# A spatial gate by one Strassen level, logits summed on TensorE, and engine orders written out as lists

## The chip, the core and the metric

The kernel runs on one core of one Trainium2 chip. The time is the device time of one execution in microseconds (us): the median of three runs was 236.79 us (236.54 to 237.99). The engines named below are PE (TensorE, matrix products), DVE (VectorE, elementwise), ACT (ScalarE, activations and PSUM evictions), POOL (GpSimd) and SP (SyncE, here an issuer of DMA transfers). Each engine works through its own list of instructions in order and meets the others through semaphores.

## The reference

One token sequence x of 2048 x 512 (bf16) is normalised, and two branches are added to it.

```python
xn = layernorm(x)                                   # 2048 x 512
# A: 32 heads of 16, each token looks at 8 tokens: itself, 2, 4, ... 14 back
q, k, v = split(xn @ wqkv)
logits  = sum_d q[s] * k[s - 2w] / 4                # w = 0..7, masked below token 0
A = (softmax_w(logits) @ v[s - 2w]) @ wo
# B: gated MLP with a spatial matrix w_sp (2048 x 2048)
z  = gelu(xn @ w_in)                                # 2048 x 1792
z1, z2 = z[:, :896], layernorm(z[:, 896:])
g  = w_sp @ z2 + b_sp[:, None]                      # 2048 x 896
B  = (z1 * g) @ w_out
out = x + A + B
```

The largest product is w_sp @ z2: 2048 x 2048 x 896.

## The kernel before, in words

Python code builds a list of tasks (`T(engine, function, reads, writes, est, name)`), finds their dependences from the tiles they read and write, and a planner (`schedule`) sets the order on each engine from estimated durations, priorities and four short prefixes. `emit` then writes each engine's instructions in that order with semaphore waits. All large tiles lie in one SBUF tensor, `arena`; the eight PSUM banks are the tensor `ps`.

The work in stages, with the lines that the profile names:

- **Start.** Nine dummy matmuls (L570) while x arrives. Each of 16 token blocks of 128 goes through DVE statistics (L598, L601), a power on POOL for 1/sqrt (L603) and the DVE normalisation (L605). Blocks 0 to 3 are transposed on PE (L620), the others by a DMA transpose (L609), into xnT.
- **Projections.** For each of four column blocks j of 512 tokens: Q and K with features on partitions (L665, evicted two banks at once by ACT at L673), V with tokens on partitions (L647, L651, stored to a DRAM scratch at L654), and z2 (L785, gelu with accumulated sums at L790, squares at L812, statistics at L818 to L828, power on POOL L831, normalisation on DVE L834). The last 16 columns of K are copied by POOL (L679) as a halo for the next block. z1 is computed with features on partitions (L802, L807).
- **Logits.** For each j DVE multiplies Q with eight shifted K views, one chunk of four feature groups at a time (L689, 128 x 4096), adds the four products in three adds (L694), a DMA transpose of 1 MB (L706) turns features to the free axis, and two more DVE adds finish the sum over features (L714, L717). The softmax follows (L727 to L766, the exponential on ACT at L746). The attention weights go to DRAM and back (L768, L772 on POOL's queue) to change their token order.
- **Gate.** Four transposing loads of w_sp, 512 output tokens each, 2 MB (L841), two buffers. For each of 7 feature groups and 4 token groups: ACT writes the bias to a PSUM bank (L902), 16 matmuls of 128 x 512 add the product (L908), and DVE multiplies the bank into z1 (L915).
- **Attention output.** For each j and parity, ACT's queue loads nine shifted views of V from DRAM, DVE multiplies them by the weights (L933), adds them (L937 twice, L941), and SP issues a DMA transpose (L946).
- **Output.** For each token block ACT writes x into a PSUM bank (L969), 4 + 7 matmuls add A and B (L974, L978), ACT evicts (L987), and ACT's queue stores.

The names in the new lists follow the tasks: `P1_3` is product 1 of token-block pair 3, `lg2_1` the second logits sum of block j = 2.

Of the kernel before, what the change touches and what calls it, by code (L numbers as in the profile page):

```python
# [14 lines left out]
class Plan:  # L15
# [79 lines left out]
    def schedule(self, lookahead=64, slack=120.0, dma_bw=300.0, xbar_bw=190.0,  # L95
                 dma_lat=1700.0, issue_ns=None, inv_tol=None, sw_bias=1300.0, verbose=False):
        inv_tol = inv_tol or {"dve": 2400.0}
        issue_ns = issue_ns or {"sp": 650.0, "act": 650.0, "pool": 660.0}
        pending = {e: {} for e in ENGS}
        for t in self.tasks:  # L100
            pending[t.eng].setdefault(t.prio[0], []).append(t)
        for e in ENGS:
            for c in pending[e]:
                pending[e][c].sort(key=lambda t: t.prio)
        byname = {t.name: t for t in self.tasks}
        before = {}
        for names in self.orders:
            for a, b in zip(names, names[1:]):
                assert byname[a].eng == byname[b].eng
                before.setdefault(byname[b], []).append(byname[a])  # L110
        eng_free = {e: 0.0 for e in ENGS}
        dma_free = {e: 0.0 for e in ENGS}
        dma_glob = [0.0]
        order = {e: [] for e in ENGS}
        remaining = len(self.tasks)

        def lat(d, t):
            if d.dma is not None:
                return 150.0
            if d.eng == t.eng:  # L120
                return 35.0
            return 210.0 if d.eng == "pe" else 80.0

        cur_tbl = [None]

        def dur(t):
            if t.dma is not None:
                return issue_ns.get(t.eng, 650.0)
            if t.tbl is not None and t.tbl != cur_tbl[0]:
                return t.est + 1300.0  # L130
            return t.est

        while remaining:
            best = None
            for e in ENGS:
                pl = []
                for c in pending[e]:
                    pl.extend(pending[e][c][:lookahead])
                if not pl:
                    continue  # L140
                cands = []
                for t in pl:
                    ok = all(p.start is not None for p in before.get(t, ()))
                    ready = 0.0
                    for d in t.deps:
                        if d.end is None:
                            ok = False
                            break
                        r = d.end + lat(d, t)
                        if r > ready:  # L150
                            ready = r
                    if ok:
                        st_ = max(eng_free[e], ready + t.margin)
                        if t.tbl is not None and t.tbl != cur_tbl[0] and cur_tbl[0] is not None:
                            st_ += sw_bias
                        cands.append((st_, t))
                if not cands:
                    continue
                pick = None
                pool_c = list(cands)  # L160
                while pool_c:
                    mn = min(c[0] for c in pool_c)
                    near = [c for c in pool_c if c[0] <= mn + slack]
                    P = min(near, key=lambda c: (c[1].prio, c[0]))
                    pend = P[0] + dur(P[1])
                    viol = False
                    for c in cands:
                        if c[1].prio[0] < P[1].prio[0] and pend > c[0] + inv_tol.get(e, 300.0):
                            viol = True
                            break  # L170
                    if not viol:
                        pick = P
                        break
                    pool_c.remove(P)
                if pick is None:
                    pick = min(cands, key=lambda c: (c[1].prio[0], c[0], c[1].prio))
                if best is None or (pick[0], pick[1].prio) < (best[0], best[1].prio):
                    best = pick
            if best is None:
                raise RuntimeError("scheduler stuck (dependency cycle?)")  # L180
            st, t = best
            e = t.eng
            if t.tbl is not None and t.tbl != cur_tbl[0] and cur_tbl[0] is not None:
                st -= sw_bias
            t.start = st
            if t.dma is not None:
                iss = issue_ns.get(e, 650.0)
                t.eng_end = st + iss
                bw = xbar_bw if t.dma.get("xbar") else dma_bw
                xs = max(st + 0.5 * iss, dma_glob[0])  # L190
                xe = xs + t.dma["nbytes"] / bw
                dma_glob[0] = xe
                t.end = max(xe, st + iss) + dma_lat
            else:
                t.eng_end = st + dur(t)
                t.end = t.eng_end
                if t.tbl is not None:
                    cur_tbl[0] = t.tbl
            eng_free[e] = t.eng_end
            pending[e][t.prio[0]].remove(t)  # L200
            order[e].append(t)
            remaining -= 1
        self.order = order
        self.makespan = max(t.end for t in self.tasks)
        if verbose:
            self.report()
        return order

    def report(self, buckets=10):
        print("makespan(est) = %.1f us" % (self.makespan / 1000.0))  # L210
        for e in ENGS:
            busy = sum((t.eng_end - t.start) for t in self.order[e])
            last = max((t.eng_end for t in self.order[e]), default=0.0)
            print("  %-4s tasks=%5d busy=%7.1f us (%.0f%%) last_end=%7.1f us" % (
                e, len(self.order[e]), busy / 1000.0, 100.0 * busy / max(self.makespan, 1.0), last / 1000.0))
# [90 lines left out]
DEFAULT_CFG = dict(  # L306
    xdma=4,
    fill=1,
    warm=9,
    fill0=2,  # L310
    perm=0,
# [3 lines left out]
def build_kernel(nc, A_x, A_wqkv, A_wo, B_x, B_w_in, B_w_sp, B_b_sp, B_w_out, out, report=False, sched_kw=None,  # L315
# [4 lines left out]
    assert D == 512 and S % 512 == 0  # L320
    NB = S // 128
    NJ = S // 512
    FH = 896
    HF = FH // 2
    FC = FH // 128
    W = 8
    KP = 16
    FILL = cfg["fill"]
    XDMA = cfg["xdma"]
    PERM = cfg["perm"]  # L330
# [4 lines left out]
    ascr = nc.dram_tensor("ascr", (S, 256), BF).ap()  # L335
# [9 lines left out]
    WSL = NB * 512  # L345
    NWS = min(2, NJ)
    NPB = 4
    NQ = 2
    off = {}
    base = 0  # L350
    for k, v in dict(xin=0, xn=2048, wqk=4096, wv_raw=8192, xin2=10240, Vn=12288).items():
        off[k] = base + v
    off["wT"] = base
    base += NWS * WSL
    off["OT"] = base
    off["xnT"] = base
    base += 4 * S
    off["w_in"] = base
    off["w_out"] = base
    off["wo"] = base + FC * 512  # L360
    base += 7168
    off["QT"] = base
    off["KT"] = base + 4 * 512 * NQ
    ksz = 2 * 4 * (512 + KP)
    off["pb"] = off["KT"] + ksz
    off["Vs"] = off["QT"]
    off["On"] = off["pb"]
    off["xres"] = off["On"] + 2048
    off["yout"] = off["xres"] + 2048
    base = off["pb"] + NPB * 4096  # L370
    off["Ve"] = base
    base += 9216
    off["zeros"] = base
    off["Za"] = base
    off["sqj"] = base + 512
    base += 512 + FH
    for name, n in (("z2", NB * FH), ("z1T", FC * S), ("attn", NB * 256), ("R", 128), ("ident", 128),
                    ("maskt", 256), ("mx", 128), ("Zb", 256), ("bbc", S)):
        off[name] = base
        base += n  # L380
        base = (base + 15) & ~15
    ARENA_E = base
# [3 lines left out]
    for name, n in (("prime", 4), ("Z", 128), ("st6", NB * 9),  # L386
                    ("mv", NB * 2), ("vpe", NB), ("rstd", NB), ("s1", 2 * NB), ("s2", NB), ("m2", NB), ("msq", NB),
                    ("vpe2", NB), ("rstd2", NB), ("mhalf", 4)):
        foff[name] = fb
        fb += n  # L390
# [4 lines left out]
    with ExitStack() as es:  # L395
# [13 lines left out]
        def AC(o_, dims):  # L409
            return bass.AP(tensor=ar, offset=o_, ap=[[AR, 128]] + [list(d) for d in dims])  # L410
# [10 lines left out]
        def bank(k):  # L421
            return ps[:, 512 * k: 512 * (k + 1)]
# [17 lines left out]
        for s_ in range(NPB):  # L440
            R1(("pb", s_), "pb", 4096, 4096 * s_)
        for s_ in range(2):
            R1(("On", s_), "On", 1024, 1024 * s_)
# [625 lines left out]
```

## Time and profile before

| | |
|---|---|
| median of three runs | 236.79 us |
| span of the profiled execution, first to last instruction | 236.3 us |
| granted TensorE clock | 1.000 in every window |
| PE busy | 230.9 us, 98% of the span |
| DVE busy | 202.8 us, 86% |
| ACT busy | 117.6 us, 50% |
| POOL busy | 51.8 us, 22% |
| DMA | 41.75 MB in 87,021 packets, mean 177 GB/s |
| first gate matmul | 97.3 us |
| last matmul | about 233.9 us |

The profile gives the span of one execution and no other time for it; the median of the runs is 0.5 us above that span. "Busy" of PE counts modelled ends of pipelined matmuls: one 512-column matmul is listed with 379 ns, but 32 of them in a row take 6.91 us, so one is issued every 216 ns. Where work is summed, the distance from start to start is used, not the listed duration. In a list of groups, the last columns are busy time and mean of one, then the idle time of the engine just ahead of them and who ended it.

### The profile page before, as it was taken

Reading aid. Unit: us, or ns where it says so; the run is one execution under the profiler, and the core shown is the slowest. Engines: PE = TensorE matmul, PEld = TensorE weight load, DVE = VectorE, ACT = ScalarE, POOL = GpSimd, SP = SyncE. Lnnn points to the kernel's source line nnn. Section 1 sums busy time; section 2 is a strip of 40 time slices with the busy share of each in tenths; the row PEclk is TensorE's granted clock in tenths of the full one; section 3 lists DMA queues with packets and bytes.
Section 4 is the critical chain, followed back from the end, with each engine's and each line's share of the span. In section 5 each row is a group of like instructions: output and inputs, shape, how many; then the busy total and the mean of one; then the engine's idle time right before and its main releaser. Section 6 shows DMA issues by size and latency. Waiting matters only on the chain.

```text
span 236.3 us, 2933 instructions
## 1 busy us (share of the span) xinstructions
PE 230.9 (98%) x1094; PEld 109.9 (47%) x1094; DVE 202.8 (86%) x230; ACT 117.6 (50%) x227; POOL 51.8 (22%) x67
## 2 busy tenths in 40 slices
PE   8999999999999999999999999999999799999995
PEld 2454454554554444444444444444444344444553
DVE  4789969998989989997999991799999999999900
ACT  2798488988988978942012132134124134111441
POOL 4447963771690050001301000001000000000000
DMA  6999986290209899696549999999773959912132
GB/s 226 281 356 189 206 223 192 92 178 0 90 3 178 202 249 260 116 247 214 147 96 242 199 215 232 248 182 337 191 206 93 243 147 275 223 23 44 67 89 67
DMA packets 87021, 41.75 MB, mean 177 GB/s; under 512 B 66000, under 2 KB 85856, under 8 KB 87008
## 3 DMA queue, kind: packets, MB, share of 16 engines
q1 hardware_dynamic: 70928, 23.24, 48.4%
q10 hardware_dynamic: 14640, 14.13, 20.4%
q0 software_dynamic: 1440, 4.21, 6.6%
q8 instruction: 8, 0.13, 0.2%
q14 instruction: 5, 0.04, 0.0%
HBM read 20.05 MB, written 5.26 MB: 107 GB/s over the span
## 4 chain that ended last, share of the span: by engine, by line
DVE 50%; PE 31%; DMA 9%; POOL 5%; issue 2%; ACT 2%; DVEq 0%
DVE arena L689 11%; DVE arena L694 9%; DMA arena<-arena 9%; PE ps L908 9%; PE ps L978 6%; DVE arena L933 6%; DVE arena L937 4%; DVE arena L915 4%; POOL fpool L831 4%; PE ps L974 4%; PE ps L665 4%; PE ps L647 3%; PE ps L785 3%; DVE arena L834 2%; DVE arena L717 2%
## 5 line engine op out<-in xcount | busy, mean ns | idle before, releaser
L908 PE MATMUL ps<-arena 128*128 128x512 bf16 x448 | 97.5, 379 | 0.0
L908 PEld LDWEIGHTS ps<-arena 128*128 128x128 bf16 x448 | 43.9, 98 | 52.8 <-ACT ps L902 0.2
L902 ACT ACTIVATE ps<-arena 128x512 f32<-128x512 bf16 x28 | 16.5, 599 | 62.2 <-DVE arena L915 62.1
L933 DVE TENSOR_TENSOR arena<-arena 128x4096 bf16<-128x4096 bf16 x16 | 36.3, 2285 | 0.4
L689 DVE TENSOR_TENSOR arena<-arena 128x4096 bf16<-128x4096 bf16 x16 | 36.1, 2285 | 0.2
L937 DVE TENSOR_TENSOR arena<-arena 128x4096 bf16<-128x4096 bf16 (+1 forms) x16 | 28.1, 1754 | 0.3
L665 PE MATMUL ps<-arena 128*128 128x512 bf16 x128 | 28.3, 379 | 0.0
L694 DVE TENSOR_TENSOR arena<-arena 128x4096 bf16<-128x4096 bf16 x12 | 27.5, 2288 | 0.2
L978 PE MATMUL ps<-arena 128*128 128x512 bf16 (+2 forms) x119 | 27.0, 366 | 0.0
L785 PE MATMUL ps<-arena 128*128 128x448 bf16 x128 | 25.5, 353 | 0.2 <-DVE arena L630 0.2
L802 PE MATMUL ps<-arena 128*128 128x512 bf16 x112 | 24.3, 379 | 0.0
L665 PEld LDWEIGHTS ps<-arena 128*128 128x128 bf16 x128 | 14.5, 113 | 13.1
L915 DVE TENSOR_TENSOR arena<-ps,arena 128x512 bf16<-128x512 f32 x28 | 19.1, 680 | 0.0
L673 ACT ACTIVATE arena<-ps 128x1024 bf16<-128x1024 f32 x16 | 16.3, 1021 | 5.3 <-PE ps L665 4.9
L987 ACT ACTIVATE arena<-ps 128x512 bf16<-128x512 f32 (+1 forms) x16 | 9.4, 585 | 18.4 <-PE ps L978 17.0
L790 ACT ACTIVATE arena<-ps 128x448 bf16<-128x448 f32 x32 | 17.3, 542 | 2.4
L978 PEld LDWEIGHTS ps<-arena 128*128 128x128 bf16 x119 | 13.2, 113 | 11.3
L974 PE MATMUL ps<-arena 128*128 128x512 bf16 (+2 forms) x68 | 16.6, 366 | 1.6 <-DMA arena<-arena 1.6
L785 PEld LDWEIGHTS ps<-arena 128*128 128x128 bf16 x128 | 12.3, 98 | 12.0 <-ACT arena L626 0.7
L807 ACT ACTIVATE arena<-ps 128x512 bf16<-128x512 f32 x28 | 15.9, 595 | 3.2 <-PE ps L802 2.7
L802 PEld LDWEIGHTS ps<-arena 128*128 128x128 bf16 x112 | 10.9, 98 | 13.2
L679 POOL COPY arena<-arena 128x16 bf16<-128x16 bf16 x12 | 14.4, 1207 | 10.9 <-DVE arena L689 9.2
(61 smaller groups left out, 191.2 us busy)
## 6 DMA issues: line engine op xcount, KB each, us to landing
arena<-vscr ACTq DMA_DIRECT2D x8, 1152.0 KB, 7.5
arena<-in_A_x_dram ACTq DMA_DIRECT2D x17, 128.0 KB, 6.0
vscr<-arena POOLq DMA_DIRECT2D x16, 128.0 KB, 2.3
arena<-in_A_x_dram SPq DMA_DIRECT2D x15, 128.0 KB, 4.6
out_dram<-arena ACTq DMA_DIRECT2D x15, 128.0 KB, 1.9
arena<-in_A_wqkv_dram SPq DMA_DIRECT2D x3, 512.0 KB, 5.4
ascr<-arena POOLq DMA_DIRECT2D x4, 256.0 KB, 4.1
arena<-ascr POOLq DMA_DIRECT2D x4, 256.0 KB, 3.5
```

Of the source, the lines that this page charges most:

```text
L665: last = t.matmul(bank(k + which), AC(off["wqk"] + 1024 * dc + col0, [[4, 128]]), AC(off["xnT"] + dc * S + 512 * j, [[1, 512]]), start=(dc ...
L689: T("dve", lambda v: v.tensor_tensor(pbv, qb, kb, ALU.mult), reads=[("QT", c, j), ("KT", c, j), ("KTpad", c, j)], writes=[("pb", s_)], est ...
L694: T("dve", lambda v: v.tensor_tensor(A("pb", 4096, 4096 * a), A("pb", 4096, 4096 * a), A("pb", 4096, 4096 * b), ALU.add), reads=[("pb", b) ...
L785: last = t.matmul(ps[:, 512 * k: 512 * k + HF], AC(off["xnT"] + dc * S + 128 * b, [[1, 128]]), AC(off["w_in"] + 1792 * dc + c0, [[1, HF]]) ...
L790: T("act", (lambda k, hf: lambda a: a.activation(A("z2", HF, FH * b + HF * hf), ps[:, 512 * k: 512 * k + HF], ACTF.Gelu_apprx_tanh, accum_ ...
L802: lastm = t.matmul(bank(k), AC(off["w_in"] + 1792 * dc + 128 * fc, [[1, 128]]), AC(off["xnT"] + dc * S + 512 * j, [[1, 512]]), start=(dc = ...
L908: last = t.matmul(bank(k), AC(off["z2"] + FH * sh + 128 * fc, [[1, 128]]), AC(off["wT"] + WSL * r_ + sh * 512, [[1, 512]]), start=False, s ...
L915: T("dve", lambda v: v.tensor_tensor(uv, bank(k), uv, ALU.mult), reads=[("ps", k)], writes=[("z1T", fc, tc)], est=c_dve(512) + 20, name="u ...
L933: T("dve", (lambda iv, tv, av: lambda v: v.tensor_tensor(tv, iv, av, ALU.mult))(iv, tv, av), reads=[("attn", j), ("Ve", par)], writes=[("V ...
L937: T("dve", (lambda n: lambda v: v.tensor_tensor(AC(off["Vs"], [[4096, 2], [1, n]]), AC(off["Vs"], [[4096, 2], [1, n]]), AC(off["Vs"] + n, ...
L974: t.matmul(po, AC(off["OT"] + 512 * ot_pos(tb) + 128 * cc, [[1, 128]]), AC(off["wo"] + 512 * cc + c0, [[1, n]]), start=False, stop=False, ...
L978: last = t.matmul(po, AC(off["z1T"] + fc * S + t0, [[ts, 128]]), AC(off["w_out"] + 512 * fc + c0, [[1, n]]), start=False, stop=(fc == FC - ...
```

## The change

What it does, part by part:

1. **Order.** The planner is removed. `ORDERS` holds one list of task names for each engine, and `follow` takes them as they stand.
2. **Gate.** The product w_sp @ z2 is done by one level of Strassen's scheme (Winograd's form): the 2 x 2 blocks of w_sp (token halves) and z2 (token halves by feature halves) give 7 products instead of 8. Tokens are on partitions: for each of 8 pairs of token blocks, 7 products `P1` to `P7` of 8 matmuls, 128 x 448 each. DVE forms the sums of w_sp blocks for each pair (`S13`, `S2`, `S4`) and of z2 blocks once (`T1` to `T4`, two groups each), ACT moves partial sums between banks and SBUF (`fk`, `S5`, `S2e`, `Sc`, `S3e`, `g11`, `g21`), DVE adds (`h`), ACT adds the bias (`g12`, `g22`). w_sp comes in 16 transposing loads of 0.5 MB.
3. **z1 and u.** z1 is computed with tokens on partitions too, both halves evicted in one gelu. DVE multiplies in SBUF (`u`, 128 x 896 bf16, 16 times), and SP issues a DMA transpose of each result (`uT`), which the output matmuls read.
4. **Logits.** Two of the three adds for each j stay. The sums over the 128 partitions of a chunk are taken by PE with a 0/1 mask of 32 columns, eight matmuls of 512 columns at four column positions (`lg`), into banks 6 and 7. ACT evicts (`lge`), a DMA transpose of 256 KB (`lgT`) puts tokens on partitions in the order the weights need, so the way through DRAM and L714, L717 go.
5. **Smaller.** z2's gelu takes both halves at once; V tasks are paired; the working PSUM ring has six banks; b_sp is loaded as a 4 KB column tile by POOL (`ldbsp`) and converted by DVE (`bspf`).

```diff
-    def schedule(self, lookahead=64, slack=120.0, ...):
...
+    def follow(self, orders):
+        byname = {t.name: t for t in self.tasks}
+        self.order = {e: [byname[n] for n in orders[e]] for e in ENGS}
...
+ORDERS = dict(
+    pe="""
+warm xTr0 fill0 z2_0_0 xTr1 z2_0_1 z2_1_0 xTr2 z2_1_1 xTr3 z2_2_0 z2_2_1 Q0_0 K0_0 Q0_1 K0_1 z2_3_0 z2_3_1 Q0_3
...
+z2_10_0 z2_8_1 z2_10_1 z2_9_1 z2_9_0 z2_11_1 lg2_0 z2_11_0 V13 V12 Q3_0 V15 K3_0 V14 K3_1 Q3_1 lg2_1 K3_3 Q3_3
+K3_2 z2_12_1 z2_12_0 Q3_2 z2_14_0 z2_14_1 z2_13_1 z2_15_1 z2_13_0 lg3_0 z2_15_0 z1_8_1 z1_8_0 z1_0_1 z1_0_0
+z1_2_0 z1_1_1 z1_10_1 z1_10_0 z1_1_0 z1_2_1 lg3_1 z1_11_0 z1_9_1 z1_9_0 z1_11_1 z1_3_0 z1_3_1 z1_6_0 z1_6_1
+z1_12_1 z1_4_0 z1_4_1 z1_12_0 z1_13_0 z1_14_0 z1_13_1 z1_14_1 z1_5_1 z1_5_0 z1_7_1 z1_7_0 z1_15_0 z1_15_1 P1_0
+P1_1 P5_0 P2_0 P3_0 P5_1 P6_0 P2_1 P7_0 P6_1 P4_0 P7_1 P3_1 P1_2 P1_3 P4_1 P2_2 P6_2 P5_2 P7_2 P3_2 out0_0 P4_2
+P5_3 P2_3 P6_3 P1_4 P3_3 P7_3 out8_0 P6_4 P4_3 P5_4 P2_4 P1_5 out10_0 P7_4 P3_4 P4_4 out2_0 P1_6 P2_5 P6_5 P5_5
...
+    dve="""
+steps0 steps1 zeros bspf bnst0 bnag0 bnst1 norm0 bnag1 xTf0 norm1 bnst2 bnag2 bnst3 norm2 bnag3 bnst5 bnag5
...
+ssub0 zm2 sm3_1 ze2 zv1 ssub1 prod3_1 prod3_0 zq2 zv0 zv2 padd3_1 prod3_2 prod3_3 sz1_0 zn2 sz2_0 zn10 zn6 zn4
+S13_0 zn7 sz3_0 padd3_3 sz1_1 zn3 zn0 srec0 sz2_1 S2_0 zn1 zm3 zn8 zn5 T1_0 sz3_1 T1_1 zn9 zn11 zq3 sattn0 sm1_2
+pv0_0_0 ze3 sm2_2 zv3 sm3_2 S13_1 S4_0 pv0_0_1 zn15 zn14 zn12 zn13 pva2048_0_0 T3_0 T3_1 T2_0 ssub2 T2_1 S2_1
+pva1024_0_0 T4_0 sz1_2 S4_1 srec1 sz2_2 T4_1 h_0 sattn1 sm1_3 sz3_2 srec2 pvc0_0 sattn2 u_0 pv2_0_1 u_8 S13_2
...
+    pool="""
+ldbsp mhalf ident0 ident1 Vzero rstd0 rstd1 rstd2 rstd3 ktpad mlog0 rstd5 rstd4 mlog1 halo0_0 rstd7 rstd6 mask0
...
+            def msum(s_, first, last, n):
+                def mm(t):
+                    for w in range(8):
+                        g, hb = w % 4, w // 4
+                        lm = t.matmul(ps[32 * g: 32 * g + 32, 512 * (6 + hb): 512 * (6 + hb) + 512], mlog,
+                                      A("pb", 512, 4096 * s_ + 512 * w), start=first, stop=last,
+                                      skip_group_check=True, tile_position=(0, 32 * g))
...
+            prod("P1", ba, w0, lambda s: z2m(s, 0), True, [A11] + zr(0, 0))
+            evac("fk", bank(bb, HF), ba, ("ps", bb), scale=-1.0)
+            prod("P5", bc, s0, tm(0), True, [("S1", r_), ("T1", 0), ("T1", 1)])
+            evac("S5", A("Y", HF, HF), bc, ("Y", 1), scale=-1.0)
+            prod("P2", ba, w0 + 1024, lambda s: z2m(8 + s, 0), False, [A12] + zr(8, 0))
+            evac("g11", gz(0), ba, ("G", r_, 0), bias=bt)
+            prod("P6", bb, s0 + 1024, tm(1), False, [("S2", r_), ("T2", 0), ("T2", 1)])
+            evac("S2e", A("X", HF), bb, ("X", 0), scale=-1.0)
+            prod("P3", bc, s0 + 2048, lambda s: z2m(8 + s, 1), False, [("S4", r_)] + zr(8, 1))
+            evac("Sc", A("Y", HF), bc, ("Y", 0))
+            prod("P7", bb, w0 + 2048, lambda s: z2m(s, 1), False, [A21] + zr(0, 1))
+            evac("S3e", A("X", HF, HF), bb, ("X", 1))
...
+            prod("P4", bb, w0 + 3072, tm(2), False, [A22, ("T4", 0), ("T4", 1)])
+            evac("g21", gz(2), bb, ("G", r_, 2), bias=bbm)
```

In `prod`, each product is 8 matmuls of 448 columns into one bank; `evac` is one ACT instruction of 448 columns. SP's new list has the pieces in this order from the gate on: `lgT3 ldwo0 ldwout ldwo1 wT2_0 wT3_0 wT2_1 OTd0_0 ldwo2 uT_0 ldwo3 uT_8 wT3_1 wT4_0 wT4_1 OTd2_0 uT_10 wT5_0 wT5_1 ...`.

More of the change, by code (lines that the diff above doesn't have):

```diff
@@ L93, in add @@
         return t
[L95 to L104, printed above, removed]
-        byname = {t.name: t for t in self.tasks}
[L106 to L134, printed above, removed]
-            for e in ENGS:
[L136 to L172, printed above, removed]
-                        break
[L174 to L215, printed above, removed]
+    def follow(self, orders):
+        byname = {t.name: t for t in self.tasks}
+        assert len(byname) == len(self.tasks) == sum(len(o) for o in orders.values())
+        self.order = {e: [byname[n] for n in orders[e]] for e in ENGS}
+        at = {e: 0 for e in ENGS}
+        k = 0
+        while any(at[e] < len(self.order[e]) for e in ENGS):
+            moved = False
+            for e in ENGS:
+                while at[e] < len(self.order[e]):
+                    t = self.order[e][at[e]]
+                    assert t.eng == e
+                    if any(d.start is None for d in t.deps):
+                        break
+                    t.start = t.end = t.eng_end = float(k)
+                    k += 1
+                    at[e] += 1
+                    moved = True
+            assert moved, "the orders wait for one another"
+        self.makespan = 0.0
@@ L439, in build_kernel @@
                 R(("KT", c, j), "sb", [(k_off(c, j), k_off(c, j) + 512)])
-        for s_ in range(NPB):
+        for s_ in range(3):
             R1(("pb", s_), "pb", 4096, 4096 * s_)
@@ L560, in build_kernel @@
                 name="ld%s" % ("qk"[which]))
-        for b in range(4, min(8, NB)):
+        for b in range(4, 8):
             ld_x(b, "sp", after=[("w_in2a", 0)])
@@ L1021, in build_kernel @@
+        pj, pq = pairs[7]
+        out_block(4 * pj + pq, 14 % 4)
+        out_block(4 * (pj + 2) + pq, 15 % 4, parts=(384, 128))
+        plan.follow(ORDERS)
         if not emit:
```

702 lines of the change are left out of this document (408 added, 294 removed).

## The prediction

> **What bounds the kernel now.** I read the busy times of the page first, then PE's timeline (start, length, idle time in brackets), the groups, and the windows of 10 us.
>
> ```profile
> PE 230.9 (98%) x1094; PEld 109.9 (47%) x1094; DVE 202.8 (86%) x230; ACT 117.6 (50%) x227; POOL 51.8 (22%) x67
> ```
> ```profile
> 10.46 3.19 PE L785 MATMUL ps<-arena 128*128 128x448 bf16 x16
> 13.49 7.07 PE L665 MATMUL ps<-arena 128*128 128x512 bf16 x32
> ...
> 97.26 55.42 PE L908 MATMUL ps<-arena 128*128 128x512 bf16 x256
> ...
> 189.25 1.02 PE L974 MATMUL ps<-arena 128*128 128x512 bf16 x4 [1.61 <-DMA arena<-arena]
> ```
>
> PE's pieces join without gaps. Its idle time is 1.18 us at the start, 0.19 us at 6.3 us and the 1.61 us shown: 3.0 in all. 230.9 + 3.0 + 2.4 (from the last matmul's end at 233.9 us to the span's end) = 236.3 us, so PE's list is the time. DVE is second at 86%, but nothing that PE waits for comes from it, except at the first blocks.
>
> ```profile
> L908 PE MATMUL ps<-arena 128*128 128x512 bf16 x448 | 97.5, 379 | 0.0
> L689 DVE TENSOR_TENSOR arena<-arena 128x4096 bf16<-128x4096 bf16 x16 | 36.1, 2285 | 0.2
> L694 DVE TENSOR_TENSOR arena<-arena 128x4096 bf16<-128x4096 bf16 x12 | 27.5, 2288 | 0.2
> L915 DVE TENSOR_TENSOR arena<-ps,arena 128x512 bf16<-128x512 f32 x28 | 19.1, 680 | 0.0
> ```
> ```profile
> 0.00:10.00 10.00, 8.63 (x39) 3.62 (x39) 6.04 (x17) 4.00 (x9) 4.05 (x14) 1.00 0.78 232
> 10.00:20.00 10.00, 10.00 (x53) 5.25 (x52) 8.43 (x21) 9.71 (x23) 5.66 (x9) 1.00 1.14 341
> 20.00:30.00 10.00, 10.00 (x48) 4.79 (x47) 8.67 (x25) 6.10 (x11) 8.15 (x15) 1.00 1.01 188
> 30.00:40.00 10.00, 10.00 (x52) 5.18 (x51) 8.21 (x7) 8.36 (x19) 4.77 (x6) 1.00 0.83 227
> ```
>
> In the windows the third pair of numbers is DVE's. DVE is idle for 4.0, 1.6, 1.3 and 1.8 us here and for 2.4 us from 40 to 80 us: 11.1 in all. PE does not feel it.
>
> **PE's work after.** From the chain of waits, which gives pieces from start to start, 32 matmuls of 512 columns take 6.91 us from start to start (216 ns each), 16 of 448 columns 3.03 us (189.4 ns). The gate goes from 448 of the first (96.7 us) to 7 x 8 x 8 = 448 of the second (84.9 us): -11.9. z1 goes from 112 x 216 ns to 128 x 189.4 ns: 24.2 both. Projections and output keep their matmuls. The eight mask sums (`lg`) are new, and no row shows a matmul at a column position. Eight matmuls of 512 columns take 1.73 us one after another, 0.43 us four at a time; I take 0.5 us, near the low end because the four positions write separate partitions, and keep 1.73 for a rival. That adds 4.0 us: 222.2 us in the end.
>
> [...]
>
> **DVE's work after.** Goes: 4 of 12 adds L694 (9.0 us from start to start), L714 and L717 (9.8), 28 multiplies L915 (0.60 us each from start to start, 16.8), small ones 0.5. Comes: `u`, 16 x 0.56 us, and `h`, 8 x 0.58 us (128 x 896, between the bf16 rows of 512 with 0.42 us and of 1024 with 0.69 us): 13.6; T sums, 8 x 1.05 us (1792 elements, between 0.69 and the 1.22 us of 2048): 8.4; `S13`, 8 x 1.18: 9.4; `S2` and `S4`, 16 x 0.65: 10.4. Net +6, so 209 us. ACT loses L902 (16.5) and some 7 us of fixed cost in gelus, and gains 72 evictions of about 0.55 us (row L790: 0.54) and 4 `lge` of 1.02 us (row L673): about 138 us, no bound.
>
> **The wait that decides.** PE's list now holds instructions that wait for DVE: each `lg` for an add, `P5`, `P6`, `P3`, `P4` for sums. I add up both lists to the places where they meet. Up to the end of `padd3_3`, which `lg3_1` needs, DVE has 16 blocks of statistics and normalisation (19.0 us), start-up (1.1), 16 products and 8 adds of 2.25 us (54.0), softmax heads and pieces of tails (4.8), z2 statistics and five normalisations (4.1) and one `S13` (1.2): 84.1 us. The same unit times give 76.3 us for what DVE did before 89.2 us in this trace; its busy time there is 77.0. PE has 82.2 us in front of `lg3_1`, plus 2.7 us idle (1.4 at the start as now, 1.3 from the late start below). So if DVE idles by more than 0.8 us up to there, PE waits for it. Later meetings follow within 2 us: `T4_1` ends at 115.6 us of DVE's list, and `P4_0` starts at 114.5 us of PE's.
>
> Hence: DVE's 84.1 us, plus its idle time d, plus PE's list from `lg3_1` on (0.5 + 22 z1 halves of 0.757 = 16.7 + 56 products of 1.515 = 84.8 + output 38.1 = 140.0), plus the tail of 2.4.
>
> For d: of the 11.1 us before, 1.9 were waits for the power L831, which the new lists fill with other work, and 0.7 for ACT's squares, placed earlier too; about half of the 2.7 us behind L603 goes likewise. That leaves 7.1. The list then puts `bspf` ahead of the first statistics, and it waits for `ldbsp`, POOL's first transfer. POOL's tiny store landed after 3.9 us, the V stores after 2.0 at best; issued at 0.7 us, b_sp lands between 2.7 and 4.6, where x landed at 3.1. So -0.4 to +1.5. Against it, statistics of blocks 5, 9, 10 are moved ahead to fill waits for x, some 1 us. I take d = 7.0, bounds 5 and 10.
>
> ```profile
> DMA to landing us min/median/max: 3.9/3.9/3.9
> ```
>
> That is the tiny store's line (L517, 16 KB). The next is from the view of the halo copies:
>
> ```profile
> L679 POOL COPY arena<-arena x12: 187/1183/2318, 19.1 to 65.4; 128x16 bf16<-128x16 bf16 x12
> ```
>
> It is why d can be 10: a POOL copy takes 0.19 us alone and up to 2.32 us beside a DVE product, and the new POOL list puts copies and mask instructions ahead of `rstd9`, `rstd11`, `rstd10`, `rstd8`, which DVE needs. [...]
>
> **Sum:** 84.1 + 7.0 + 140.0 + 2.4 = 233.5 us of span; with the 0.5 us between this profile's span and the median, **234.0 us**, 1.2% faster. d from 5 to 10 gives 232.0 to 237.0. About 1% is what a measurement of this kernel tells from no change; that line lies at 234.4, or d = 7.4.
>
> What hides the rest: the gate leaves 2.6 us of spare DVE time per pair (PE 7 x 1.515 + 2 x 2.375 = 15.4 us; DVE sums 2.5, `h` and `u` 1.7, attention 8.6). The DRAM trip of the weights and the 6.7 us that DVE waited for L706 go, and are worth nothing: PE never waited for them. After DVE's end at 209 + 7 us, a transpose (3.0 to 4.0 us in the rows of L946) and two output blocks follow, still short of PE's end.
>
> **Rivals.**
> 1. *PE sets the pace again.* The lists keep DVE's idle time near the 4.0 us of the first window alone: 84.1 + 4.0 + 140.0 + 2.4 + 0.5 = 231.0. Floor, with no DVE wait: 222.2 + 2.7 + 2.4 + 0.5 = 227.8. For it: gaps behind POOL and x can be filled. Against it: 5 us of gaps from 10 to 40 us now. Range 229.5 to 232.
> 2. *The column positions do not run side by side*, and the Strassen gain goes into the sums: `lg3_1` starts after 82.2 + 7 x 1.23 + 2.7 = 93.5 us, later than DVE's 91.1; 93.5 + 141.2 + 2.4 + 0.5 = 237.6. Nothing in this trace speaks on it.
> 3. *Slower: w_sp pieces land late.* A piece's buffer is free after `P4` of two pairs earlier; up to its `S13` there are 6.1 to 9.2 us by the two lists (pair 4: from 136 to 142.3). The load is now 0.5 MB. The view of the loads before:
>
> ```profile
> L841 SPq DMA_TRANSPOSE arena<-in_B_w_sp_dram x4: 7637/9328/11357, 76.8 to 145.8; - x4
> ...
> DMA to landing us min/median/max: 10.0/13.0/16.0
> ```
>
> The 2 MB loads land after 10.0 at best; the 256 KB transposes of L946 after 4.0 in the median and 10.2 at worst. A quarter of the former should need 4 to 6 us, but SP issues them between `uT`s that wait for DVE, and the gate now carries 12 MB of transposes in some 125 us, where it carried 8 MB in 139. Beyond 6.2 + 2.6 = 8.8 us from release to landing every us is paid in each of six pairs: at 10.0 us, 1.2 x 6 = 7.2, so 241; at 11, 247. Range 239 to 248.
>
> **How the numbers follow.** Forecast (232 to 237) 0.50: 0.27 below 234.4, 0.23 above. Rival 1 0.17, rival 2 0.08, rival 3 0.17; the other 0.08, half of it below 232 and half above 237, for unit times I got wrong. Faster by over 1%: 0.27 + 0.17 + 0.04 = 0.48. Slower by over 1% (above 239.2): rival 3's 0.16, 0.01 of rival 2 and 0.03 of the rest = 0.20. Within 1%: 0.32. The range 229.5 to 241.5 leaves out about half of rival 3 and of the unknown rest, under 0.15.
>
> **What would show it.** Right: PE idle about 11 us in the first 100, ended by DVE's adds and products (`lg`) and by T sums; hardly any from 130 us on; gate matmuls at 189 ns; eight mask matmuls in under 0.8 us; the first statistics behind `bspf`. Wrong: PE's total idle near 4 us (rival 1), mask matmuls 216 ns apart (rival 2), or DVE idle before `S13`, ended by DMA (rival 3).

## The result

| | before | changed |
|---|---|---|
| median | 236.66 us (236.46 to 237.99, 4 runs) | 266.43 us (264.26 to 267.79, 4 runs) |
| span of the profiled execution | 236.3 us | 266.0 us (its time 267.79) |
| PE busy | 230.9 us | 237.1 us |
| ACT busy | 117.6 us | 154.7 us |
| first gate matmul | 97.3 us | 131.4 us |

The changed kernel is slower by 12.3%: ratio 1.1227, 95% interval 1.1158 to 1.1295. The forecast was 234.0 us, in a range of 229.5 to 241.5. Medians and ratios of the versions below are taken over their fast runs alone, those within 1.5% of the version's fastest, and the ranges over all runs. From the first gate matmul to the end the changed kernel takes 134.6 us where it took 139.0: the gate starts 34 us late, and of the 12 us that it should save, 4.4 arrive.

The page of the changed kernel, busy times and the granted clock in 40 slices of 6.65 us:

```profile
PE 237.1 (89%) x1159; PEld 114.8 (43%) x1174; DVE 202.8 (76%) x243; ACT 154.7 (58%) x233; POOL 52.8 (20%) x63
...
PEclk9999999879979979997999999869999999999999
```

DVE's 202.8 us lie below the forecast's 209. ACT is 17 us above its 138, and the clock, full in every window before, dips six times, to 0.50 to 0.55 in windows of 2 us, once behind each of the six longest waits shown or named below. The groups of the same page, busy time and mean first, then idle time ahead and its releaser, and behind them the row of the page of before that the forecast priced `lge` by:

```profile
L898 PE MATMUL ps<-arena 128*128 128x448 bf16 x448 | 88.6, 357 | 7.3 <-DVE arena L869 6.5
L784 PE MATMUL ps<-arena 128*128 128x448 bf16 x256 | 59.7, 391 | 12.2 <-ACT arena L671 7.4
...
L720 ACT ACTIVATE arena<-ps 128x1024 bf16<-128x1024 f32 x4 | 19.1, 4765 | 0.0
```
```profile
L673 ACT ACTIVATE arena<-ps 128x1024 bf16<-128x1024 f32 x16 | 16.3, 1021 | 5.3 <-PE ps L665 4.9
```

L720 is `lge`, the eviction of the logits: 4.77 us each, 19.1 in all. The forecast had 1.02 each, after another eviction of the same size. PE's idle time is now put down to DVE and ACT, where the table of before has 0.0. PE's timeline of the changed kernel (start, length, instruction, idle time ahead in brackets):

```profile
49.63 0.93 PE L784 MATMUL ps<-arena 128*128 128x448 bf16 x4 [2.71 <-ACT arena L671]
...
74.31 4.13 PE L784 MATMUL ps<-arena 128*128 128x448 bf16 x12 [2.72 <-ACT arena L671]
94.36 5.64 PE L784 MATMUL ps<-arena 128*128 128x448 bf16 x20 [1.97 <-ACT arena L671]
...
122.11 9.44 PE L784 MATMUL ps<-arena 128*128 128x448 bf16 x40 [2.90 <-ACT arena L795]
173.72 10.92 PE L898 MATMUL ps<-arena 128*128 128x448 bf16 x48 [6.50 <-DVE arena L869]
```

Each of the four waits on ACT ends some 5.6 us after an `lge` has started: behind it in ACT's list stand the next Q, K or z evictions, which start 4.2 us after it each time, 3.7 us later than planned, and until they have run PE has no free bank. The last wait is of another kind. Left out of these lines is one more of 2.08 us at 56.55, ended by an x transpose. The chain of waits of the changed kernel (start, length, what) holds both kinds, and one piece of good news:

```profile
66.17 0.55 PE ps L704 x8
...
68.77 4.64 ACT arena L720
...
158.04 13.93 DMA arena<-in_B_w_sp_dram
```

Eight mask matmuls take 0.55 us. An `lge` of 4.6 us follows on the chain itself. And one w_sp piece of 0.5 MB, `wT3_1`, landed 13.9 us after its issue. The view of all 16 pieces:

```profile
L859 SPq DMA_TRANSPOSE arena<-in_B_w_sp_dram x16: 1903/2402/9397, 74.7 to 220.2; - x16
...
DMA to landing us min/median/max: 4.4/5.1/13.9
```

The median of 5.1 us is inside the forecast's 4 to 6. The piece of 13.9 was issued at 158.04, and at 158.83 ACT's queue issued a load of shifted V views (`ldVe2_1`, 1.15 MB), which took 13.5 us itself. It was not the only one: four of the 16 pieces ran beside a V load for 5 us or more, and they landed after 8.8, 13.9, 12.0 and 11.6 us (issued at 137.6, 158.0, 162.0 and 208.8); the other twelve took 4.4 to 6.2. DVE had to wait for one of the four. The last two rows come from the list of waits of the changed kernel: in total, times, longest.

```profile
DVE arena L869 <- DMA arena<-in_B_w_sp_dram: 10.8, 1, 10.8
...
DVE fpool L1021 <- DMA arena<-in_B_b_sp_dram: 3.8, 1, 3.8
```

The first is `S13` of pair 3, for which DVE stood still 10.8 us, and PE 6.5. The second is `bspf`, which waits for b_sp (issued at 1.33 us, landed 3.83 us later); behind it the first statistics start at 5.36 us (3.07 before).

### The profile page after: what moved, and what is told of

The parts are those of the page before. It is cut to its first block, busy times and chain, and to the rows that moved or that the text cites. A ratio compares the mean times of both kernels' runs of the same rounds, so it can differ in the third digit from the quotient of the medians.

```text
span 266.0 us, 3151 instructions
## 1 busy us (share of the span) xinstructions
PE 237.1 (89%) x1159; PEld 114.8 (43%) x1174; DVE 202.8 (76%) x243; ACT 154.7 (58%) x233; POOL 52.8 (20%) x63
## 4 chain that ended last, share of the span: by engine, by line
PE 67%; ACT 14%; DMA 9%; DVE 5%; issue 3%; ACTq 1%; POOL 0%; DVEq 0%; POOLq 0%
PE ps L898 29%; PE ps L784 13%; PE ps L1000 9%; PE ps L663 7%; ACT arena L720 6%; DMA arena<-in_B_w_sp_dram 5%; PE ps L996 5%; PE ps L640 3%; ACT arena L795 3%; ACT arena L671 2%; DMA arena<-arena 2%; DVE arena L689 2%; DMA arena<-in_B_b_sp_dram 1%; ACTq L983 1%; PE ps L704 1%
## 5 line engine op out<-in xcount | busy, mean ns | idle before, releaser
L898 PE MATMUL ps<-arena 128*128 128x448 bf16 x448 | 88.6, 357 | 7.3 <-DVE arena L869 6.5
L784 PE MATMUL ps<-arena 128*128 128x448 bf16 x256 | 59.7, 391 | 12.2 <-ACT arena L671 7.4
L898 PEld LDWEIGHTS ps<-arena 128*128 128x128 bf16 x448 | 44.2, 99 | 50.4 <-DVE arena L869 6.9
L689 DVE TENSOR_TENSOR arena<-arena 128x4096 bf16<-128x4096 bf16 x16 | 36.5, 2285 | 16.8 <-ACT arena L671 12.3
L784 PEld LDWEIGHTS ps<-arena 128*128 128x128 bf16 x256 | 28.0, 114 | 41.4 <-issue 9.5
L959 DVE TENSOR_TENSOR arena<-arena 128x4096 bf16<-128x4096 bf16 x16 | 36.2, 2285 | 2.1 <-DMA arena<-vscr 2.1
L795 ACT ACTIVATE arena<-ps 128x896 bf16<-128x896 f32 x32 | 29.2, 932 | 12.8 <-PE ps L784 12.7
L663 PE MATMUL ps<-arena 128*128 128x512 bf16 x124 | 30.6, 385 | 2.4 <-DMA arena<-arena 2.1
L1000 PE MATMUL ps<-arena 128*128 128x512 bf16 (+2 forms) x118 | 26.9, 366 | 0.1
L671 ACT ACTIVATE arena<-ps 128x1024 bf16<-128x1024 f32 x16 | 17.5, 1092 | 10.5 <-PE ps L663 10.5
L663 PEld LDWEIGHTS ps<-arena 128*128 128x128 bf16 x128 | 14.2, 114 | 16.5 <-issue 4.4
L677 POOL COPY arena<-arena 128x16 bf16<-128x16 bf16 x12 | 16.5, 1386 | 23.0 <-ACT arena L671 23.0
L720 ACT ACTIVATE arena<-ps 128x1024 bf16<-128x1024 f32 x4 | 19.1, 4765 | 0.0
L695 DVE TENSOR_TENSOR arena<-arena 128x4096 bf16<-128x4096 bf16 x8 | 18.2, 2277 | 0.0
L869 DVE TENSOR_TENSOR arena<-arena 128x2048 bf16<-128x2048 bf16 x8 | 9.8, 1225 | 11.0 <-DMA arena<-in_B_w_sp_dram 10.8
L640 PE MATMUL ps<-arena 128*128 128x512 bf16 x61 | 17.0, 411 | 0.4 <-issue 0.2
L596 POOL TENSOR_TENSOR fpool<-fpool 128x1 f32<-128x1 f32 x16 | 15.8, 988 | 6.1 <-DVE fpool L594 5.9
L1000 PEld LDWEIGHTS ps<-arena 128*128 128x128 bf16 x119 | 11.4, 98 | 12.8
L996 PE MATMUL ps<-arena 128*128 128x512 bf16 (+2 forms) x61 | 15.1, 365 | 0.4
```

Of the source, the lines that this page charges most:

```text
L640: last = t.matmul(bank(k + i), AC(off["xnT"] + dc * S + 128 * (b + i), [[1, 128]]), AC(off["wv_raw"] + 512 * dc, [[1, 512]]), start=(dc == ...
L663: last = t.matmul(bank(k + which), AC(off["wqk"] + 1024 * dc + col0, [[4, 128]]), AC(off["xnT"] + dc * S + 512 * j, [[1, 512]]), start=(dc ...
L671: T("act", lambda a: a.activation(AC(qo, [[ko - qo, 2], [1, 512]]), ps[:, 512 * k: 512 * k + 1024].rearrange("p (t n) -> p t n", t=2), ACT ...
L689: T("dve", lambda v: v.tensor_tensor(pbv, qb, kb, ALU.mult), reads=[("QT", c, j), ("KT", c, j), ("KTpad", c, j)], writes=[("pb", s_)], est ...
L720: T("act", lambda a: a.activation(AC(off["stage"], [[128, 2], [1, 128], [256, 4]]), PC(512 * 6, [[512, 2], [4, 128], [1, 4]]), ACTF.Copy), ...
L784: last = t.matmul(bank(k + hf, HF), AC(off["xnT"] + dc * S + t0, [[ts, 128]]), AC(off["w_in"] + 1792 * dc + c0, [[1, HF]]), start=(dc == 0 ...
```

## The experiments

Theory: three separate causes, namely the writing order of `lge`, V loads beside transposing transfers, and the late start. Rival: the lock-step of DVE and PE that the prediction built its sum on. The edit to `lge` (e1, and in e8 and e9 once more) changes code; all others move names in the lists, and the lists' line breaks go with it, so line numbers differ by up to 33 from kernel to kernel.

**e1: `lge` written densely.** The bank holds 4 groups of logits per key in turn; the change reads it as it stands and writes 4 elements 512 bytes apart. The edit writes 128 adjacent elements and steps in the read instead.

```diff
-AC(off["stage"], [[128, 2], [1, 128], [256, 4]]), PC(512 * 6, [[512, 2], [4, 128], [1, 4]])
+AC(off["stage"], [[128, 2], [256, 4], [1, 128]]), PC(512 * 6, [[512, 2], [1, 4], [4, 128]])
```

> The changed kernel with one edit: the ACT eviction of the logits sums (L720) walks its 1024 elements so that 128 neighbouring ones are written in a row, instead of four elements 512 bytes apart; the same values land in the same places. Theory (scattered writes): L720 falls from 4.76 us to 1.0 to 1.1 us, like the other 1024-element evictions; the four stalls of PE behind it and the low clock after them go; the first gate product starts near 112 us instead of 131.5, and the time is 245 to 251. Rival (the list lag between DVE, POOL and PE sets the first half, and L720 only lies beside it): L720 falls but the time stays above 260. Second rival (reading every fourth PSUM element costs as much): L720 stays near 4.8 us and the time near 266.

Measured: 250.64 us (248.92 to 252.93, 4 runs), ratio 1.0591 (1.0499 to 1.0683): 15.8 us less than the change, at the upper end of the theory's 245 to 251. The first gate matmul starts at 115.8 us. The view of the eviction's line in e1:

```profile
L720 ACT ACTIVATE arena<-ps x4: 1014/1026/1045, 42.9 to 105.8; 128x1024 bf16<-128x1024 f32 x4
```

The same elements from the same banks into the same place: 1.03 us, though the read now steps. Of the four long waits on ACT one of 1.50 us is left, with another cause (the exponential `sexp1`, with a table load of 1.28 us on either side). The wait for `wT3_1` stays, 9.7 us of DVE and 5.97 of PE, and the one ended by an x transpose has grown from 2.08 to 4.10 us.

**e2: `ldVe2_1` later**, everything else as in the change.

```diff
-act: ... g11_2 S2e_2 ldVe2_1 S5_2 ... g21_2 S5_3 ldxr9 ...
+act: ... g11_2 S2e_2 S5_2 ... g21_2 S5_3 ldVe2_1 ldxr9 ...
```

> The changed kernel with one load of V views (ldVe2_1, 1.15 MB) issued ten ACT instructions later, behind S5_3. In the profile it was issued 0.8 us after the w_sp piece that DVE then waited 10.8 us for, and that piece took 13.9 us to land. Theory (two transfers share the DMA engines): the piece lands in 5 to 6 us, DVE waits under 3 us for it, and the time falls by 7 to 10 us, to 256 to 259. Rival (transposing loads queue behind each other on SP's queue, whatever ACT's queue does): landing stays above 10 us and the time stays within 2 us of 266.

Measured: 261.2 us (259.32 to 264.18, 4 runs), ratio 1.109 (1.1024 to 1.1155), 5.2 us less than the change, where the theory had 7 to 10 and 256 to 259. `wT3_1` now lands after 5.4 us, as the theory has it. The waits of e2:

```profile
DVE arena L857 <- DMA arena<-in_B_w_sp_dram: 2.7, 2, 1.6
```

10.8 us have become 2.7, and PE's wait of 6.5 is gone. In its place the transfer `OTd2_0` of attention output holds PE for 1.79 us: issued 0.45 us behind `ldVe2_1`, it takes 8.7 us (median 4.4). That is where a part of the theory's gain went.

**e3: the bias column later** (`ldbsp` behind `rstd3` on POOL, `bspf` behind `norm7` on DVE).

```diff
-pool: ldbsp mhalf ident0 ... rstd2 rstd3 ktpad          dve: steps1 zeros bspf bnst0 ... norm7 prod0_1
+pool: mhalf ident0 ... rstd2 rstd3 ldbsp ktpad          dve: steps1 zeros bnst0 ... norm7 bspf prod0_1
```

> The changed kernel with the 4 KB load of b_sp behind rstd3 in POOL's list and its conversion behind norm7 in DVE's. Theory: the first statistics start at 3.1 to 3.4 us instead of 5.4, the first block product on PE some 2 us earlier, and 1 to 2 us of it reach the end: 264 to 265.5. Rival (hidden by later waits): start earlier, end within 0.7 us of 266.

Measured, one execution: 262.7 us, 3.7 below the change's median and 1.6 below its fastest run, so the size of this gain is rough; the theory had 264 to 265.5. The wait is gone and the first statistics start at 2.96 us; DVE's wait for w_sp stays, 11.5 us.

**e4: all three.**

> The three edits of the runs before it together. Theory (three separate causes explain the miss): the time comes back to the forecast of the prediction, 232 to 240. Rival (a further cause in the lists, such as waits of PE for DVE): above 242, with the rest of PE's idle time in the first half ended by DVE or POOL.

Measured: 243.76 us (243.25 to 248.56, 4 runs), ratio 1.0319 (1.0265 to 1.0373). One by one the edits were worth 15.8, 5.2 and 3.7, 24.7 us; together 22.7. Within the scatter of these versions, some 2 us, they add up, so the three causes are nearly independent. But e4 is still 3.2% slower than the kernel before: above 242, as the rival has it, though what holds PE is neither DVE nor POOL. PE's timeline of e4 has two long waits on transfers:

```profile
50.50 3.39 PE L634 MATMUL ps<-arena 128*128 128x512 bf16 x8 [4.75 <-DMA arena<-arena]
...
160.07 1.02 PE L967 MATMUL ps<-arena 128*128 128x512 bf16 x4 [1.66 <-DMA arena<-arena]
```

The first waits for `xTd8`, issued at 42.16 us, 0.6 us ahead of the V load `ldVe0_0`. The view of the x transposes in e4:

```profile
L573 SPq DMA_TRANSPOSE arena<-arena x12: 1190/1266/1825, 14.2 to 63.9; - x12
...
DMA to landing us min/median/max: 2.4/2.5/8.1
```

The second waits for `OTd2_0`, issued at 151.33 us, 8.6 us to its landing; `ldVe2_1` was issued at 150.88 and `ldVe1_0` at 156.48.

**e5: e4 with `ldVe0_0` 35 us later.**

```diff
-act: ... z2s4 ldVe0_0 z2g5 ... sexp1 z2g14 z2g13 ...
+act: ... z2s4 z2g5 ... sexp1 z2g14 ldVe0_0 z2g13 ...
```

> As e4, with the first V load (ldVe0_0, 1.15 MB on ACT's queue, issued at 42.78 us in e4, 0.6 us behind the transposing transfer xTd8) moved some 46 us later, behind z2g14. Theory (a V load beside a transposing transfer makes that transfer slow): the slowest xTd lands in under 4 us (8.1 in e4), PE's wait of 4.75 us on it shrinks to under 2 (its norm is still late), the slow clock behind it goes too; 4 to 6 us less than e4, about 239. Rival (the transfer is slow or late for what stands ahead of it on SP's queue, lgT0, and for rstd8 behind POOL's copies): the landing stays at 6 to 8 us, the wait at 4 to 5, the time at 244 to 245. A second rival: the transfer lands early, but DVE's products hold PE instead (the lock-step of the prediction); then PE idles 2 to 4 us on DVE adds and the gain is 1 to 3 us.

Measured: 238.64 us (236.67 to 242.23, 10 runs), ratio 1.0054 (1.0001 to 1.0107), 5.1 less than e4. `xTd8` lands after 2.9 us and PE's wait of 4.75 us is gone altogether, as the theory has it; both rivals are out. (Of the x transposes one still takes 6.3 us, issued at 14.3 us among the start-up loads with no V load near; nothing waits for it.) The second wait grew from 1.66 to 2.93 us, still beside `ldVe2_1`.

**e6: e4 with `xTd8` ahead of `lgT0`** in SP's list; the V load stays.

```diff
-sp: ... xTd9 lgT0 xTd8 xTd13 ...
+sp: ... xTd9 xTd8 lgT0 xTd13 ...
```

> As e4, with one transfer moved by one place in SP's list: xTd8 ahead of lgT0; the V load stays where it was. xTd8 can then be issued at about 41 us, as its norm ends, 1.8 us ahead of the V load. Theory (what slows it is the V load): it is mostly through when the V load starts and lands in 2.5 to 4 us, or, if it needs 2.5 us and is caught by the V load for the last 0.7, in 4 to 6; PE's wait of 4.75 us falls to 0 to 2 us and the time to 239 to 242. What lands late instead is lgT0, which is then beside the V load, and no PE work waits for that one. Rival (lgT0 on the same queue made it slow): xTd8 lands in 2.5 us whatever the V load does, and e5 shows no gain.

Measured: 242.71 us (242.29 to 244.27, 4 runs), ratio 1.0275 (1.0228 to 1.0323), 1.1 less than e4, above the theory's 239 to 242 by 0.7. `xTd8` lands after 3.2 us and PE no longer waits for it. But in PE's timeline of e6 there are new, smaller waits:

```profile
53.45 1.05 PE L630 MATMUL ps<-arena 128*128 128x512 bf16 x4 [0.84 <-ACT arena L613]
55.52 0.61 PE L671 MATMUL ps<-arena 128*32 128x512 bf16 x8 [1.01 <-DVE arena L662]
...
63.84 0.62 PE L671 MATMUL ps<-arena 128*32 128x512 bf16 x8 [0.56 <-DVE arena L662]
```

`lgT0` is now the transfer beside the V load and needs 6.5 us (3.2 at the median). The expectation said that no PE work waits for it, and missed DVE's list: the mask add `smask` waits 3.4 us for it, DVE's products and adds are queued behind it, and PE waits for those (1.01 and 0.56 us). The wait of 0.84 us has another carrier: ACT stood still 2.83 us for a store of V on POOL's queue, issued at 45.6 us, which took 6.0 us (2.5 at the median; 2.0 at the same place in e7, where no V load is near). So a plain store beside the V load was slow too. Later in e6 `OTd2_0` holds PE for 3.04 us and a w_sp piece for 1.45, which is a part of why this edit gains less than e5's. With the V load left in its place the slow transfer is another one; e5's edit takes the damage away.

What the transfers got beside each other is in the view of the DMA queues. Of the changed kernel, from 158.8 to 172 us, while `ldVe2_1` (ACT's queue, q10) runs beside the w_sp pieces (SP's queue, q1); the rows give packets, MB and share of 16 engines:

```profile
DMA packets 4592, 2.12 MB, mean 161 GB/s; under 512 B 3356, under 2 KB 4591, under 8 KB 4591
...
q1 hardware_dynamic: 3423, 0.92, 68.7%
q10 hardware_dynamic: 1168, 1.18, 41.9%
```

From 143.5 to 156 us, without a V load, the core moved 175 GB/s, of which q1 154. Beside the V load the sum was 161 GB/s, with 70 for q1, less than half of what it had, and 89 for q10. What divides it between the two queues is not shown.

**e7: e5 and e6 together, `ldVe2_1` behind `sexp3`, `ldVe1_0` behind `g11_3`.**

```diff
-act: ... S5_3 ldVe2_1 ldxr9 S2e_3 sexp3 g12_2 ldVe1_0 g22_2 ... ldxr1 g11_3 ldxr11 ...
+act: ... S5_3 ldxr9 S2e_3 sexp3 ldVe2_1 g12_2 g22_2 ... ldxr1 g11_3 ldVe1_0 ldxr11 ...
```

> As e4, with both edits of e5 and e6, and the later V loads set clear of the transfers that PE waits for: ldVe2_1 from 150.9 to behind sexp3 (about 155), ldVe1_0 from 156.5 to behind g11_3 (about 163). Theory (what is left between e4 and the forecast is three V loads beside transfers on PE's path): the waits of 4.75 and 1.66 us go, with the slow clock of about 1.9 us behind the first; 241.5 - 8.3 = 233.2 of span if nothing else gets late, 233 to 237, so the same as the kernel before or up to 1.5% faster. Rival (the lock-step of DVE and PE is next): PE idles on DVE's products and adds ahead of lg3_1 instead, 3 to 5 us, and the time stays at 238 to 241, slower than before by 0.5 to 2%.

Measured: 236.02 us (235.44 to 237.01, 10 runs) against 236.58 (236.19 to 238.27, 18 runs): ratio 0.9973 (0.9953 to 0.9992). This is the one version that is not slower than the kernel before; it gains 0.3%. The time lies in the theory's 233 to 237, and the rival's waits for DVE did not come: 0.48 us behind the start. The page of e7, and two lines of PE's timeline:

```profile
PE 224.4 (96%) x1174; PEld 111.5 (48%) x1174; DVE 202.6 (87%) x243; ACT 139.9 (60%) x233; POOL 56.2 (24%) x63
...
PEclk9999999999999999999999999999999999999999
```
```profile
81.50 7.76 PE L751 MATMUL ps<-arena 128*128 128x448 bf16 x40 [1.50 <-ACT arena L762]
171.50 7.74 PE L865 MATMUL ps<-arena 128*128 128x448 bf16 x40 [0.85 <-DMA arena<-in_B_w_sp_dram]
```

No wait of PE is longer than 1.5 us, and its idle time is 6.7 us in all. PE's busy time is 12.7 us less than in the change, for the same matmuls (15 of whose records are missing there): the six dips of the clock, some 2 us each (the mean clock was 0.955, 0.999 in e7), account for it; they are in the listed durations, not in the idle time. 224.4 + 6.7 + 2.4 (from the last matmul to the end) = 233.5, the span of 233.6.

**e8 and e9: what makes the eviction slow.** Based on e7; `lge` is split into two halves of 512 elements, and each of the four `lge` uses another order of the same elements. In e8 runs of r = 2, 4, 8 and 32 adjacent elements are written before the next step of 512 bytes; in e9 single elements, a step of 4, 16, 64 and 512 bytes apart.

```diff
+# e8: r = (2, 4, 8, 32)[j]
+AC(off["stage"] + 128 * h, [[r, 128 // r], [256, 4], [1, r]]), PC(512 * (6 + h), [[4 * r, 128 // r], [1, 4], [4, r]])
+# e9: q = (2, 8, 32)[j]; the fourth as the change has it
+AC(off["stage"] + 128 * h, [[256, 4], [1, q], [q, 128 // q]]), PC(512 * (6 + h), [[1, 4], [4, q], [4 * q, 128 // q]])
```

> As e7, with each logit eviction (lge) split in two halves of 512 elements, written in runs of r adjacent elements before the next step of 512 B: r = 2 for lge0, 4 for lge1, 8 for lge2, 32 for lge3 (r = 1 is the change, r = 128 is e1 and e7). What is read off is the duration of each half. The rows so far: 1024 elements 4.76 us with r = 1 and 1.03 with r = 128, so 3.65 ns more for an element that steps. Theory (every step to another place costs the same 3.65 ns, however long the run): a half has 512/r steps over 0.6 us dense; 1.5 us with r = 2, 1.07 with 4, 0.83 with 8, 0.66 with 32. Rival (what is slow is writing less than 4 bytes in one place, so that two adjacent elements are enough): 0.6 us for all four. [...] The time of the whole kernel is to stay within 2 us of e7, as no lge grows to more than 3 us.

> As e8, but every lge half writes single elements (2 bytes) one step apart: 4 bytes in lge0, 16 in lge1, 64 in lge2, and 512 in lge3, which is the order of the change cut into halves. Theory after e8 (a lone 2-byte write is slow, wherever the next one goes): all four halves take about 2.4 us (half of 4.76). Rival (what is slow is a far step after a lone element, so that near steps are free): 0.6 us at 4 and 16 bytes, 2.4 at 512. lge3 is the control and takes 2.4 by both. By the theory ACT has 3 x 3.6 us more than e7 ahead of the first V's, and the whole kernel lands near 245 to 255; by the rival it stays within 4 us of e7.

ACT's timeline of e8, both halves of a `lge` in one row; r = 2 and 32 are shown, 4 and 8 take 1.08 and 1.11 us:

```profile
40.26 1.11 ACT L690 ACTIVATE arena<-ps 128x512 bf16<-128x512 f32 x2
...
97.17 1.09 ACT L690 ACTIVATE arena<-ps 128x512 bf16<-128x512 f32 x2
```

and of e9, steps of 4, 16, 64 and 512 bytes:

```profile
39.66 1.34 ACT L692 ACTIVATE arena<-ps 128x512 bf16<-128x512 f32 x2
...
55.90 4.74 ACT L692 ACTIVATE arena<-ps 128x512 bf16<-128x512 f32 x2
...
75.80 4.76 ACT L692 ACTIVATE arena<-ps 128x512 bf16<-128x512 f32 x2
...
103.64 4.76 ACT L692 ACTIVATE arena<-ps 128x512 bf16<-128x512 f32 x2
```

In e8 two adjacent elements are already enough, as its rival has it: the theory of a price per step falls, for runs of 2 are not slow. In e9 both expectations fail at one end each. Single elements 4 bytes apart cost little more than dense ones (1.34 us for both halves), against the theory that a lone 2-byte write is slow anywhere; at 16 bytes the full price is there, against the rival that near steps are free. So neither the far step nor the lone element is slow by itself; slow were single elements 16, 64 and 512 bytes apart (8 bytes were not run). The price is 4.6 ns an element instead of about 1. It belongs to the write: the fourth `lge` of e9 reads its bank without steps and is slow, and all of e8 reads with steps and is fast. A half took 0.54 to 0.56 us in runs of 2 or more, 0.67 in single elements 4 bytes apart, and 2.4 at 16, 64 and 512. Why 16 bytes are too far and 4 are not is not shown.

e8 took 237.44 us in its one execution, e9 247.38: the four `lge` of e9 take 15.6 us together where e7's take 4.1, and the time is 11.4 us longer than e7's.

## Why the prediction was wrong, point by point

**The step that failed** is a term of the sum of DVE's and ACT's work: "4 `lge` of 1.02 us (row L673): about 138 us, no bound". Row L673 has the same number of elements and writes them densely. The term measured 4.76 us, 3.74 more, four times: 15.0 us on ACT. PE's four waits behind it add up to 10.3 us, each with a dip of the clock behind it, and without it the kernel is 15.8 us shorter (e1). The mistake was to take a duration by element count where the diff shows the output pattern. And "no bound", read off the sum of ACT's work, says nothing of a single instruction on a list worked through in order: ACT is 58% busy in the changed kernel, and still PE waits for it four times.

**Rival 3, w_sp pieces late,** held in its sign but not in its mechanism. It priced a general lateness, 1.2 us in each of six pairs. The pieces take 5.1 us at the median, as estimated; four of sixteen met a V load, and one of them cost 5.2 us (e2). The prediction weighed the pieces against the `uT`s on SP's queue; the V loads on ACT's queue are in none of its terms. The trace of before had the collision. This is the view of its logits transposes, 1 MB each:

```profile
L706 SPq DMA_TRANSPOSE arena<-arena x4: 4741/4876/6296, 46.4 to 133.0; - x4
...
DMA to landing us min/median/max: 6.7/8.9/16.4
```

The two with no V load beside them landed after 6.7 us each, the two with one after 11.1 and 16.4 (other loads ran beside these too). The prediction took such spreads, 10.0 to 16.0 for w_sp and 4.0 to 10.2 for L946, as the good and the bad end of one transfer, and did not ask what ran beside the bad end.

**The same collision elsewhere** was in no term: `ldVe0_0` beside `xTd8`, 5.1 us (e5), and the V loads beside the attention output with the rest, 2.6 us (from e5 to e7). It is the same collision, found three times: with a V load moved away from one transfer, or the transfer from it, the next one beside it was slow (`OTd2_0` 8.7 us in e2, `lgT0` 6.5 in e6).

**The late start,** 1.3 us in the sum, is mis-sized: b_sp landed at 5.2 us, not by 4.6, the first statistics are 2.3 us late, and taking it away is worth about 3.7 us (e3, one execution).

**The wait that decides** is a step that failed too: the path on which the forecast's sum runs is not the one that sets the time. The sum goes through DVE's list up to `padd3_3` and has PE wait there for 6.2 us (91.1 less 82.2 and 2.7). In the changed kernel ACT and transfers hold PE ahead of the gate, not DVE. In e7, where these are out of the way, DVE's last add ends at 87.92 us with 7.3 us of idle time up to there; d was taken as 7.0, bounds 5 to 10, and held. But DVE's work up to there is 80.6 us, not 84.1, a little less in nearly every term, so `lg3_1` starts at 89.19, without a wait; behind the start DVE holds PE for 0.48 us in the whole run. Rival 1 names the engine that paces the work, PE. Its floor of 227.8 us is not reached for three reasons. PE's list is 224.4 us, where the prediction had 222.2 (its own terms, 230.9 - 11.9 + 4.0, give 223.0). PE idles 6.7 us, 2.7 in the forecast. And 1.8 us lie around the span, 0.5 in the forecast.

**From span to time.** The sum of 233.5 us of span is met by e7's 233.6, and that is luck: two errors of opposite sign, -1.9 up to `lg3_1` and +2.0 from there to the end (144.4 us for 142.4). And 0.5 us for what lies around the span was wrong: it compared one execution's span with the median of others, and the profiled one, 236.3 us, is longer than nearly all others of that kernel (most are 234.4 to 235.4). Nearly every execution here lasts 1.7 to 1.9 us longer than its own span, those of the kernel before too (236.53 for a span of 234.7). With 1.8 the sum is 235.3, and no longer faster by over 1%.

**What held:** the gate's matmuls at 189 ns (the row of 40 in e7: 7.74 us less the last one's 0.35, over 39 steps), and with it 12 us less of matmul time in the gate; column positions side by side, 0.55 us a sum (forecast 0.5), so rival 2 is out. Of the signs named for a wrong forecast one came: DVE idle before `S13`, ended by DMA, is the row of 10.8 us. None of them pointed at ACT.

Of the 32.4 us between the forecast and the measured median the three edits of e4 give back 22.7 (singly `lge` 15.8, the V load beside `wT3_1` 5.2, the late start 3.7), e5's V load 5.1 and the last moves of e7 2.6. Of the 2.0 us that are left, 1.3 are the span's surroundings. Each share is uncertain by some 2 us, for the versions scatter by that much.

## What to carry to other kernels

Take the price of an eviction from its access pattern, not from its size: with bf16 output, write adjacent elements and step in the PSUM read instead (here 1024 elements took 1.1 us in pairs, 1.3 singly at 4 bytes, 4.7 to 4.8 singly at 16 and more). Look at every large load on any queue when a transfer on PE's path is near it in time; moving four names in the lists was worth some 13 us here. And a saving on the busiest engine counts only as far as its list still runs without gaps: from the kernel before to e7, PE's busy time falls by 6.5 us and its idle time grows by 3.7.

## What the hardware showed

**An ACT write of single bf16 elements** took 4.6 ns an element at steps of 16, 64 and 512 bytes and 1.3 at 4 bytes (e9); pairs took 1.1 (e8).

**A V load of 1.15 MB on ACT's queue beside a transposing transfer on SP's:** landings of 8.1 us (median 2.5), 13.9 (5.1), 8.6 (4.0) and 6.5 (3.2) in the cases above; beside a plain store of 128 KB on POOL's queue, 6.0 (2.5).

**The clock fell to about half behind some short waits, but not behind each.** Windows of 2 us, the figure after the bracket is the granted clock; first of the changed kernel, behind its wait of 1.97 us, then of e6, behind one of 3.04 us (that one ended by a transfer):

```profile
95.00:97.00 2.00, 2.00 (x8) 0.55 0.84 160
97.00:99.00 2.00, 2.00 (x8) 0.60 1.18 264
99.00:101.00 2.00, 2.00 (x17) 1.00 0.19 68
```
```profile
159.00:161.00 2.00, 2.00 (x12) 1.00 1.38 239
```

Eight matmuls are in each of the two low windows and twelve in the full one: this dip lasted some 4 us and cost 0.45 x 2 + 0.40 x 2 = 1.7 us. Behind the wait of 2.90 us in the changed kernel the clock is 0.50; behind one of 2.72 in e3 and the one of 1.61 in the kernel before it stays full. So the length of a wait alone does not decide; what does is left open. Here a wait of 1.97 us on PE cost 3.7 in all.
